# A recurrent attention kernel: value halves at both ends of the forward projections, and five unit buffers with one buffer of key rows in the backward loop

## The chip, the cores and the metric

The kernel runs on one core of a Trainium2 chip, as one program. The metric is the time of one execution on the device in microseconds (us). Five engines work beside each other, each through its own list of instructions in order, and wait for each other by semaphores: PE (matrix products into PSUM banks), DVE and ACT (elementwise work and copies out of PSUM), POOL (a general engine) and SP, which here only issues DMAs. DMAs are also issued from ACT and POOL. "PEld" in the profile is PE's loading of the stationary operand.

## The reference

The input x (2048 tokens, width 640) is normalised to xn. Branch A is attention in 64 segments of 32 tokens, with 32 heads of 128; ahead of each segment stand 8 memory rows, which are the first 8 output rows of the segment before. Branch B is a gated MLP of width 1728. The output is x + A * silu(B). The program also computes the gradients with respect to x, mem0 and all seven weights for a given grad_out.

```python
for s in range(n_seg):                      # 64 segments, one after the other
    h = concat([mem, xn[:, 32*s:32*s+32]])  # 8 memory rows + 32 rows
    q, k, v = h @ Wq, h @ Wk, h @ Wv        # 32 heads of 128
    p = softmax(where(mask, q @ k.T * scale, -1e9))
    o = (p @ v) @ Wo
    mem = o[:, :8]                          # goes into the next segment
    outs.append(o[:, 8:])
A = concat(outs)
B = (silu(xn @ w1) * (xn @ w3)) @ w2
out = x + A * silu(B)                       # and its gradients for grad_out
```

Only the 8 memory rows depend on the segment before. The 32 body rows of q, k and v of all segments can be projected beforehand, and their attention can be done in batches.

## The kernel before

The program runs through stages: layer norm, the body rows' projections and the MLP; the first rows; the forward loop over 64 segments (`recurrence`, inner function `chain(t)`); a tail; a prologue and the backward loop over the 64 segments in reverse (`phase4_Abwd`, inner function `chain(t)`); the weight gradients. The two loops are serial: a step ends when the 8 new memory rows (forward) or their gradients (backward), turned to columns, are cast into `hx` or `gox` for the next step.

**What sets the order.** In both loops every engine is tied to the order in which the program is written (`in_order`). Batch work on body rows is put into named gaps of the step (W0, W1, V0, W2, G1 to G6) by `FILL` (forward) and by `gap` in `gap_of` (backward). Its piece is a unit (tl, qd): four heads of three segments, 96 body rows and 24 memory rows, 120 in all. A step takes 3, 3 and 2 units in turn.

**A forward step.** `packed_half(bank, hx, W, b)` (L315) is half of one projection of the memory rows into a PSUM bank, 20 matmuls of 512 columns over 32 partitions each. The banks are bA, bB and bC. `half` casts the bank into a staging tile on DVE. The order on PE is: K half 0 (bA), K half 1 (bB), gap W0, Q half 0 (bA), Q half 1 (bB), the selection of the key columns (`packed_sel`, into bC, copied into `kT`), gap W1, the selection of the query columns (into bA), gap V0, V half 0 (bB), V half 1 (bC), gap W2, the scores (L672, bA), a turning of them (L682), the softmax of the memory rows on DVE and ACT (`mmx`, `msb`, `Pm`, L684 to L693), its turning on PE (`turn_pad`, L311), the product with the value rows `vt` (L701) and the output projection `packed_out` (L339) with `fold_add` and `fold_turn`, from which `hx` of the next step is cast (L718).

The staged halves have two uses. They are written to DRAM for the backward pass by `dump` on SP (L635): keys into KS, queries and values into QVS. And the 8 value rows of each of four groups are copied from the staging tile into `vt` (L663), six copies on DVE and two on POOL. The staging tiles have the tag "stg" with two buffers: keys, queries and values take them in turn, so that the value halves go into the buffer of the keys of the same step, once the key dump has read it. The tile `oride` holds the body rows' attention output, loaded in gap W0 by SP (L870) and copied into `oTm` by POOL in gap G1 (L875); its tag, "oride", has one buffer, which `fold_add` also uses at the end of the step.

**A backward step.** `load_k(t - 1)` (L1190) loads the 8 memory and 32 body rows of keys of the next step on SP by four DMAs (L1193, L1198). They go into one of two buffers by t % 2, `krbs`: a tile `krb` and `vt`. PE reads them at L1288. Each unit has the functions `ld` (L1315: queries, values and grad rows into a `gqv` and a `gor`, probabilities into a `gPr`), `turn` (L1341, turning on PE, L1347 and L1354), `dprob`, `dsoft` and `gmem`. NG = 4 sets of buffers hold units in flight; `gmem_ld` runs `gmem` of one unit and then `ld` of the next in the list, into the set that comes free. In the prologue two further buffers serve as sets, `krb` and `vt`, six in all.

## Time and profile before

| | us |
|---|---|
| median of 3 runs (lowest, highest) | 4638.5 (4625.86, 4665.23) |
| the profiled execution, its own time | 4653.07 |
| its span | 4651.3 |
| its granted TensorE clock, share of full | 0.979 |
| forward loop, first to last cast of hx | 402.1 to 1552.1 |
| backward loop, first to last cast of gox | 1819.6 to 2851.9 |

The span lies within the profiled execution's time, and the durations come from that one execution, 14.57 us above the median of the runs. A row of a busy table gives engine, busy time and number of instructions. A row of a wait table names the instruction that waited, what released it (the engine and tile, or a DMA and what it moved), the sum of the waits, their number and the longest. A row of a timeline gives start and duration in us, the engine, the line, the operation with tiles and shapes, and in brackets the idle time before it and its releaser; x6 stands for six instructions in one row, whose duration is that from the first to the last of them. A "SPq" or "ACTq" row is a DMA issue by that engine. Where the DMA issues of a step are listed, the last figure is the time from issue to landing.

The whole span by engine, and the costliest lines of the chain of work that ended last:

```profile
## 4 chain that ended last, share of the span: by engine, by line
PE 62%; DMA 7%; DVE 5%; issue 5%; ACT 4%; SPq 1%; POOL 1%; ACTq 0%; POOLq 0%; DVEq 0%
PE bank L339 12%; PE wg L1694 11%; PE g L1675 9%; PE bank L320 7%; PE oa L1841 4%; PE wa L2229 2%; PE r6p L1625 2%; PE t6g L1657 2%; PE w2a L2085 1%; PE bank L1260 1%; PE pgxb L2162 1%; DMA kTT<-GOS 1%; DMA ggtok<-ggT 1%; PE bank L672 1%; PE bank L1288 1%
```

L339 (`packed_out`) and L320 (`packed_half`) are the products of the memory rows in the two loops; L1694 and L1675 belong to the weight gradients, which the change does not touch.

### The profile page before, as it was taken

The numbers are of one execution on the slowest core, as the hardware profiler recorded it, in microseconds if no ns is written. First come the engines' busy times: TensorE is split into PE (matmuls) and PEld (weight loads), VectorE is DVE, ScalarE is ACT, GpSimd is POOL, SyncE is SP. The second block draws the span as 40 slices with busy tenths as digits, with TensorE's granted clock in tenths as the row PEclk, the third lists the DMA queues.
The fourth block names the chain that finished last, engine by engine and source line by source line (L and its number), as shares of the span: only waits on it lengthen the run. The fifth ranks groups of instructions, "written<-read, shape, count | busy, mean of one in ns | idle before, by whom it ended". The sixth has DMA issues, their size and how long they took to land.

```text
span 4651.3 us, 155619 instructions
## 1 busy us (share of the span) xinstructions
PE 4338.8 (93%) x62336; PEld 2841.2 (61%) x62336; DVE 2277.9 (49%) x7158; ACT 1616.0 (35%) x4487; POOL 2103.7 (45%) x3531
## 2 busy tenths in 40 slices
PE   8998999999999888999999998999999999999999
PEld 4544566666656545666666665676666765667665
DVE  8734676666667534555555553243223432311550
ACT  5532555555545423333333332233223322200000
POOL 6532555555555313455554544455335543311440
PEclk9998999999999998999999999999999999999999
DMA  7773666666655668787787775655435543588783
GB/s 262 240 253 108 177 184 186 182 185 188 183 168 172 165 162 238 206 227 220 220 222 208 213 214 154 134 159 141 118 105 155 153 131 110 161 229 206 164 174 101
DMA packets 976828, 834.52 MB, mean 179 GB/s; under 512 B 518890, under 2 KB 858286, under 8 KB 974144
## 3 DMA queue, kind: packets, MB, share of 16 engines
q1 hardware_dynamic: 745319, 530.80, 41.7%
q0 software_dynamic: 129952, 228.13, 17.1%
q10 hardware_dynamic: 100835, 65.63, 5.5%
q8 instruction: 493, 8.08, 0.8%
q14 instruction: 229, 1.88, 0.1%
HBM read 472.66 MB, written 310.33 MB: 168 GB/s over the span
## 4 chain that ended last, share of the span: by engine, by line
PE 62%; DMA 7%; DVE 5%; issue 5%; ACT 4%; SPq 1%; POOL 1%; ACTq 0%; POOLq 0%; DVEq 0%
PE bank L339 12%; PE wg L1694 11%; PE g L1675 9%; PE bank L320 7%; PE oa L1841 4%; PE wa L2229 2%; PE r6p L1625 2%; PE t6g L1657 2%; PE w2a L2085 1%; PE bank L1260 1%; PE pgxb L2162 1%; DMA kTT<-GOS 1%; DMA ggtok<-ggT 1%; PE bank L672 1%; PE bank L1288 1%
## 5 line engine op out<-in xcount | busy, mean ns | idle before, releaser
L1694 PE MATMUL wg<-gr,hr 128*128 128x512 bf16 x2400 | 521.7, 379 | 0.0
L1675 PE MATMUL g<-land,ghacc 128*128 128x320 bf16 x3072 | 459.0, 300 | 0.8
L320 PEld LDWEIGHTS <-hx 128*32 128x32 bf16 x10240 | 277.9, 97 | 254.1 <-issue 28.9
L1694 PEld LDWEIGHTS <-hr 128*128 128x128 bf16 x2400 | 233.9, 98 | 278.9
L1675 PEld LDWEIGHTS <-ghacc 128*128 128x128 bf16 x3072 | 288.7, 98 | 103.7 <-ACT ghacc L92 2.2
L90 DVE CAST wgo<-wg 128x512 bf16<-128x512 f32 x72 | 49.8, 692 | 471.2 <-PE wg L1694 471.2
L339 PEld LDWEIGHTS <-gkv 128*8 128x8 bf16 x8192 | 193.9, 89 | 89.8 <-issue 2.4
L92 ACT COPY ghacc<-t6g 128x768 bf16<-128x768 bf16 (+1 forms) x176 | 137.2, 780 | 292.6 <-PE t6g L1657 284.6
L90 DVE CAST stg<-bank 128x512 bf16<-128x512 f32 x256 | 177.0, 692 | 125.2 <-PE bank L320 111.1
L1640 POOL DMA_DIRECT2D GSP<-grs x48 | 25.6, 544 | 452.6 <-ACT grs L1632 452.6
L1351 POOL DMA_DIRECT2D VTD<-gvT x176 | 130.1, 748 | 216.6 <-ACT gvT L1350 201.1
L904 POOL DMA_DIRECT2D OR<-xv x163 | 94.5, 580 | 276.8 <-ACT xv L92 241.8
L663 DVE COPY vt<-stg 8x512 bf16<-8x512 bf16 x384 | 158.9, 414 | 97.3 <-ACT stg L92 92.9
L851 POOL TENSOR_TENSOR xP<-xP,xrz 120x480 bf16<-120x480 bf16 x163 | 161.4, 993 | 87.7 <-DVE xrz L850 77.9
L1681 DVE TENSOR_TENSOR ghacc<-ghacc,g 128x320 f32<-128x320 f32 x192 | 93.6, 487 | 209.0 <-PE g L1675 209.0
L92 ACT CAST wgo<-wg 128x512 bf16<-128x512 f32 x48 | 28.1, 586 | 479.8 <-PE wg L1694 392.5
L831 ACT ACTIVATE xP<-xsp,xnm 120x120 bf16<-120x120 f32 (+1 forms) x540 | 186.0, 367 | 19.7 <-DVE xnm L813 17.6
L339 PE MATMUL bank<-Wo,oTm 128*32 128x320 bf16 x4032 | 169.8, 327 | 15.8 <-DVE oTm L90 15.5
L339 PE MATMUL bank<-WvT,gkv 128*8 128x320 bf16 x4096 | 170.3, 325 | 0.0
L320 PE MATMUL bank<-WoT,hx 128*32 128x512 bf16 x2560 | 153.5, 386 | 11.3 <-DVE hx L1309 10.9
L1398 POOL DMA_DIRECT2D GXP<-gks x157 | 92.2, 587 | 154.4 <-ACT gks L1396 149.9
L351 ACT COPY fup<-bank 64x160 f32<-64x160 f32 (+1 forms) x190 | 57.3, 334 | 300.7 <-PE bank L339 300.4
(396 smaller groups left out, 10947.7 us busy)
## 6 DMA issues: line engine op xcount, KB each, us to landing
QVS<-stg SPq DMA_DIRECT2D x128, 256.0 KB
kTT<-VTD SPq DMA_DIRECT2D x64, 320.0 KB
PR<-xP POOLq DMA_DIRECT2D x168, 120.0 KB, 3.1
VTD<-gvT POOLq DMA_DIRECT2D x168, 120.0 KB, 4.1
land<-DSR SPq DMA_DIRECT2D x168, 120.0 KB
land<-PR SPq DMA_DIRECT2D x168, 120.0 KB
OR<-xv POOLq DMA_DIRECT2D x163, 120.0 KB, 3.6
orr<-OR SPq DMA_DIRECT2D x14, 1280.0 KB
```

Of the source, the lines that this page charges most:

```text
L90: return nc.vector.tensor_copy(out, in_)
L92: return nc.scalar.copy(out, in_)
L320: k.nc.tensor.matmul(bank[32 * g:32 * g + 32, :], x[:, dc, :], W[:, dc, c0:c0 + 512], start=(dc == 0), stop=(dc == k.DC - 1), tile_positio ...
L339: k.nc.tensor.matmul(pm[a][p0:p0 + nq, 0:320], x[:, h, :], W[:, h, 320 * b:320 * b + 320], start=(first and i == 0), stop=(last and i == 1 ...
L663: (nc.gpsimd if b == 1 and g % 2 else nc.vector).tensor_copy(vt[p0:p0 + 8, c0:c0 + 512], sv[32 * g:32 * g + 8, b * 512:(b + 1) * 512])
L831: nc.scalar.activation(Pb[0:n, j, 0:n], sp[0:n, j, :], ACT.Exp, bias=nmx[0:n, j:j + 1], scale=k.scale, accum_out=Z[0:n, j:j + 1])
L851: eng.tensor_tensor(Pb[0:n, :, 0:n], Pb[0:n, :, 0:n], bc_last(rz[0:n], n), ALU.mult)
L904: q.dma_start(k.OR[120 * tl:120 * tl + n, c0:c0 + 512], v[0:n])
L1351: nc.gpsimd.dma_start(k.VTD[tl][:, :, h0:h0 + 4, :], vTq[:])
L1675: nc.tensor.matmul(pg[:], ring[:, i, j, r0:r0 + P], Ws[qd][i][:, j, 320 * h:320 * h + 320], start=(i == 0 and j == 0), stop=(i == 2 and j ...
L1694: nc.tensor.matmul(pw[:], hr[:, tl, dc * P:(dc + 1) * P], grs[i][:, tl, :], start=(tl == 0), stop=(tl == NF - 1))
L1841: nc.tensor.matmul(ac[j][i][:], orr[:, w, jj * P:(jj + 1) * P], gow[:, w, 320 * i:320 * i + 320], start=(w == 0), stop=(w == NW - 1))
```

## The change

Forward, the value projection is cut in two. V half 0 is the first product of a step (bA); ACT casts it into a new tile `sv0`, which takes the "oride" buffer, and DVE copies its four groups of value rows between the two K casts. The K and Q halves follow in other banks. V half 1 comes last (bC), into the left half of a staging tile that is still the keys' one, and its four groups (two copies on DVE, two on POOL) follow. The halves are dumped apart: the first after gap W0, the second after the products with `vt`. The oride load moves from W0 to V0, behind the dump of `sv0`, whose buffer it takes. The copy of the turned keys into `kT` goes from DVE to ACT, and `kprep` of a third unit from ACT to DVE.

Backward, key rows always go to `vt`. The tile `krb` is replaced by a tile `ub` of the same size, which holds the `gqv`, `gor` and `gPr` of a fifth set, NG = 5; the prologue keeps six sets, with one more load in its last rounds.

```diff
--- before.py
+++ after.py
@@ -623,45 +623,49 @@
             hx = hxs[t % 2]
             kT = kTs[tl % 2]
 
-            def half(W, b, sg, eng):
-                bank = (bA, bB)[b]
+            def half(W, b, sg, bank):
                 packed_half(k, bank, hx, W, b)
-                k.copy(sg[:, b * 512:(b + 1) * 512], bank[:], eng=eng)
+                nc.vector.tensor_copy(sg[:, b * 512:(b + 1) * 512], bank[:])
 
             def stage():
                 return ch.tile([P, 1024], BF16, name="stg", tag="stg", bufs=2)
 
             def dump(sg, dst, q=nc.sync):
-                q.dma_start(dst.rearrange("g r c -> (g r) c"), sg[:])
+                q.dma_start(dst.rearrange("g r c -> (g r) c"), sg)
+
+            def values(b, sv, bank):
+                packed_half(k, bank, hx, Wv, b)
+                k.copy(sv, bank[:], eng='s')
+
+            def value_rows(b, sv):
+                for g in range(4):
+                    p0, c0 = 64 * (g // 2), (g % 2) * 1024 + b * 512
+                    (nc.gpsimd if b == 1 and g % 2 else nc.vector).tensor_copy(vt[p0:p0 + 8, c0:c0 + 512], sv[32 * g:32 * g + 8])
+            sv0 = ch.tile([P, 512], BF16, name="sv0", tag="oride")[:]
+            values(0, sv0, bA)
             sk = stage()
-            half(Wk_, 0, sk, 'v')
-            half(Wk_, 1, sk, 'v')
+            half(Wk_, 0, sk, bB)
+            value_rows(0, sv0)
+            half(Wk_, 1, sk, bC)
             gap("W0")
+            dump(sv0, k.QVS[t // 4, :, :, t % 4, 1, 0:512])
             sq = stage()
-            half(Wq, 0, sq, 'v')
-            dump(sk, k.KS[t // 4, :, :, t % 4])
-            half(Wq, 1, sq, 'v')
+            half(Wq, 0, sq, bA)
+            dump(sk[:], k.KS[t // 4, :, :, t % 4])
+            half(Wq, 1, sq, bB)
             qmT = ch.tile([P, H, 8], BF16, name="qmT", tag="fup")
-            for sg, b_, dst in ((sk, bC, kT[:, :, 40 * s:40 * s + 8]), (sq, bA, qmT[:])):
+            for sg, b_, dst, eng in ((sk, bC, kT[:, :, 40 * s:40 * s + 8], 's'), (sq, bA, qmT[:], 'v')):
                 pk = bview(b_, P, 8, 4, 8)
                 packed_sel(k, pk, sg, 0)
                 packed_sel(k, pk, sg, 1)
-                nc.vector.tensor_copy(dst.rearrange("p (g j) c -> p j g c", g=4), pk[:])
+                k.copy(dst.rearrange("p (g j) c -> p j g c", g=4), pk[:], eng=eng)
                 if sg is sk:
                     gap("W1")
-            dump(sq, k.QVS[t // 4, :, :, t % 4, 0])
+            dump(sq[:], k.QVS[t // 4, :, :, t % 4, 0])
             gap("V0")
-            sv = stage()
-            packed_half(k, bB, hx, Wv, 0)
-            k.copy(sv[:, 0:512], bB[:], eng='s')
-            packed_half(k, bC, hx, Wv, 1)
-            for b in range(2):
-                if b == 1:
-                    k.copy(sv[:, 512:1024], bC[:], eng='s')
-                for g in range(4):
-                    p0, c0 = 64 * (g // 2), (g % 2) * 1024 + b * 512
-                    (nc.gpsimd if b == 1 and g % 2 else nc.vector).tensor_copy(vt[p0:p0 + 8, c0:c0 + 512],
-                                                                               sv[32 * g:32 * g + 8, b * 512:(b + 1) * 512])
+            sv1 = stage()[:, 0:512]
+            values(1, sv1, bC)
+            value_rows(1, sv1)
             gap("W2")
 
             psT = bview(bA, P, 2, 8, 16)
@@ -702,7 +706,7 @@
             om_ = oTm[:].rearrange("p (a b j) t -> p a b j t", a=2, b=2)
             for i in range(2):
                 k.copy(om_[:, :, i, :, 0:8], poms[i].rearrange("p j a q -> p a j q"), eng='vs'[i])
-            dump(sv, k.QVS[t // 4, :, :, t % 4, 1])
+            dump(sv1, k.QVS[t // 4, :, :, t % 4, 1, 512:1024])
             if t + 1 == T:
                 gap("G4")
                 gap("G5")
@@ -943,16 +947,15 @@
 
         def FILL(g, t, at, kbatch):
             kb = kbatch.get(t, ())
-            if g == "W0":
-                oride_ld(t)
-            elif g == "W1":
+            if g == "W1":
                 for u in kbatch.get(t - 1, ())[2:]:
-                    kprep(*u)
+                    kprep(*u, 'v')
                 at(pv_mm, t - 1, 1)
                 at(pv_turned, t - 1, 1)
                 at(turn_p, t - 1, 2)
             elif g == "V0":
                 at(pv_rows, t - 1, 1)
+                oride_ld(t)
             elif g == "W2":
                 ride_ld(t + 1)
                 for u in kb[0:2]:
@@ -1131,29 +1134,29 @@
                       k.FS[k.OT0:k.OT0 + k.NO, 32 * b + 8:32 * b + 32, :]))
     with tc.tile_pool(name="gst", bufs=1) as st, tc.tile_pool(name="gchain", bufs=1) as ch, \
             tc.tile_pool(name="gfill", bufs=1) as fl:
-        NG = 4
+        NG = 5
         kTs, vt, goxs, qTs, xPs, PTs, oTm = own
         kk = k.kTT
         om = oTm[:].rearrange("p h c -> p (h c)")
         two = lambda ap: ap.rearrange("p (i c) -> p i c", i=2)
         four = lambda ap: ap.rearrange("p (i c) -> p i c", i=4)
-        gors = [kk[0:120, 512 * i:512 * i + 512] for i in range(NG)]
-        gqvs = [two(ap[0:120, c:c + 1024]) for ap, c in ((kk, 2048), (kk, 4896), (kk, 5920), (om, 0))]
+        ub = st.tile([P, 2048], BF16, name="ub")
+        gors = [kk[0:120, 512 * i:512 * i + 512] for i in range(4)] + [ub[0:120, 1024:1536]]
+        gqvs = [two(ap[0:120, c:c + 1024]) for ap, c in ((kk, 2048), (kk, 4896), (kk, 5920), (om, 0), (ub, 0))]
         vTf = kk[:, 3584:4896]
         vTb = vTf[:, 0:1280].rearrange("p (h c) -> p h c", c=40)
         Qsts = [two(kk[:, c:c + 256]) for c in (3072, 3328)]
-        gPrs = [four(kk[0:120, 6944:7456])] + [x[0:120] for x in xPs]
+        gPrs = [four(kk[0:120, 6944:7456])] + [x[0:120] for x in xPs] + [four(ub[0:120, 1536:2048])]
         dSb = kk[:, 7456:7648]
         gOTs = qTs[0:2]
         gdSs = [qTs[2][0:120], PTs[0][0:120]]
         bds = [PTs[1][:, 2 * i:2 * i + 2, :].rearrange("p a (h c) -> p a h c", c=8) for i in range(2)]
-        krbs = [st.tile([P, 2048], BF16, name="krb")[:], vt[:]]
         k.fsz = st.tile([P, 448], BF16, name="gfsz")
         bdm = st.tile([P, 16, 8], BF16, name="bdm")
         b16 = st.tile([P, 16], F32, name="b16")
         xpb = st.tile([P, 8, 2, 32], F32, name="xp")
         bdf = goxs[0][:, 0:4, :].rearrange("p a b -> p (a b)").rearrange("p (a b) -> p a b", b=8)
-        for tt in gors + [t[:] for t in gOTs] + gdSs + [dSb, krbs[0], k.fsz[:]]:
+        for tt in gors + [t[:] for t in gOTs] + gdSs + [dSb, ub[:], k.fsz[:]]:
             nc.vector.memset(tt, 0.0)
         bA, bB, bC = banks
         pm = bA, bA
@@ -1188,7 +1191,7 @@
             ins[t] = vT, Pm, Qst
 
         def load_k(t):
-            kr = krbs[t % 2]
+            kr = vt[:]
             for a in range(2):
                 nc.sync.dma_start(kr[64 * a:64 * a + 8].rearrange("r (g c) -> r g c", g=2),
                                   k.KS[t // 4, 2 * a:2 * a + 2, 0:8, t % 4, :].rearrange("g r c -> r g c"))
@@ -1324,7 +1327,7 @@
                 gor = gors[g]
                 qv, Pr = gqvs[g], gPrs[g]
             else:
-                x = krbs[g - NG]
+                x = vt
                 qv = x[:, 0:1024].rearrange("p (i c) -> p i c", i=2)
                 gor = x[:, 1024:1536]
                 Pr = x[:, 1536:2048].rearrange("p (h c) -> p h c", h=4)
@@ -1495,7 +1498,7 @@
         next(work)
         for _ in range(2):
             ld_next()
-        nc.vector.memset(krbs[1][:, 1024:1536], 0.0)
+        nc.vector.memset(vt[:, 1024:1536], 0.0)
         ld_next()
         for i in range(len(pro) + 2):
             for f, o in ((turn, 0), (dprob, 1), (dsoft, 1), (gmem, 2)):
@@ -1503,7 +1506,7 @@
                     f(*pro[i - o])
                 if f is not dsoft and not (f is dprob and i % 3):
                     next(work, None)
-            if 0 <= i - 2 and (i - 2 + 6 < len(pro) or i >= len(pro) - 2):
+            if 0 <= i - 2 and (i - 2 + 6 < len(pro) or i >= len(pro) - 3):
                 ld_next()
             if 1 <= i < 17:
                 h0 = 2 * (i - 1)
```

DVE in a forward step, from the first cast of a projection to the maximum of the memory scores. bank_4107, bank_4108 and bank_4109 are bA, bB and bC. Before:

```order
L90 CAST stg<-bank_4107 128x512
L90 CAST stg<-bank_4108 128x512
L90 CAST stg<-bank_4107 128x512
L90 CAST stg<-bank_4108 128x512
L649 CAST kTT<-bank_4109 128x8x4x8
L865 COPY xPT_2984<-xpp 120x4x120
L649 CAST qmT<-bank_4107 128x8x4x8
L663 COPY vt<-stg 8x512 x6
L684 TENSOR_REDUCE mmx<-bank_4107 128x2
```

And now:

```order
L628 CAST stg<-bank_4108 128x512
L643 COPY vt<-sv_23267 8x512 x4
L628 CAST stg<-bank_4109 128x512
L628 CAST stg<-bank_4107 128x512
L628 CAST stg<-bank_4108 128x512
L90 COPY kTT<-kpt 128x12x32
L869 COPY xPT_2984<-xpp 120x4x120
L90 CAST qmT<-bank_4107 128x8x4x8
L643 COPY vt<-stg 8x512 x2
L688 TENSOR_REDUCE mmx<-bank_4107 128x2
```

Four of the six value-row copies have moved ahead of the second K cast, two are left ahead of the maximum; the key cast into kTT has gone to ACT, and the copy of a unit's keys (kpt) has come.

SP in the same step, from its first issue to the loads of a unit's keys; in brackets what each waits for (a DMA lane, or an engine's count). Before:

```order
L870 DMA oride<-OTX 128x768 [waits DMAHW2_49,DVE_49]
L635 DMA KS<-stg 128x1024 [waits DMAHW3_49,DVE_49]
L635 DMA QVS<-stg 128x1024 [waits DMAHW4_49,DVE_49]
L265 DMA kr<-KS 96x512 [waits DMAHW6_49]
L265 DMA kr<-KS 96x512 [waits DMAHW7_49,PE_49]
```

And now:

```order
L634 DMA QVS<-sv_21799 128x512 [waits DMAHW7_49,Activation_49]
L634 DMA KS<-stg 128x1024 [waits DMAHW0_49,DVE_49]
L634 DMA QVS<-stg 128x1024 [waits DMAHW1_49,DVE_49]
L874 DMA oride<-OTX 128x768 [waits DMAHW7_49,DMAHW3_49,Pool_49]
L265 DMA kr<-KS 96x512 [waits DMAHW4_49]
L265 DMA kr<-KS 96x512 [waits DMAHW5_49,PE_49]
```

The oride load has moved from the first place to behind both dumps, and it now waits for the landing of the dump of `sv0` and for POOL too.

SP in a backward step, from the load of the memory queries to the store of the score gradients. Before:

```order
L1187 DMA kTT<-QM 128x1x128 [waits DMAHW0_49]
L1193 DMA krb<-KS 8x2x1024 [waits DMAHW1_49]
L1198 DMA krb<-KS 32x2x1024 [waits DMAHW2_49]
L1193 DMA krb<-KS 8x2x1024 [waits DMAHW3_49]
L1198 DMA krb<-KS 32x2x1024 [waits DMAHW4_49]
L1299 DMA DSR<-kTT 8x16x8 [waits DMAHW5_49,DVE_49]
```

And now:

```order
L1190 DMA kTT<-QM 128x1x128 [waits DMAHW4_49]
L1196 DMA vt<-KS 8x2x1024 [waits DMAHW5_49,PE_49]
L1201 DMA vt<-KS 32x2x1024 [waits DMAHW6_49]
L1196 DMA vt<-KS 8x2x1024 [waits DMAHW7_49]
L1201 DMA vt<-KS 32x2x1024 [waits DMAHW0_49]
L1302 DMA DSR<-kTT 8x16x8 [waits DMAHW1_49,DVE_49]
```

The key loads stand at the same place and go to `vt` in every step; the first of them now waits for PE, which reads the rows of the step it is issued in.

## The prediction

> **What bounds the kernel now.** I read first the busy shares and the two loop headers, which cut the span into stages; then the busy table of the two loops; then what PE waits for in them; last the timeline of single steps. PE is busy for 93% of the span, and the change touches the two recurrent loops alone.
>
> ```profile
> PE 4338.8 (93%) x62336; PEld 2841.2 (61%) x62336; DVE 2277.9 (49%) x7158; ACT 1616.0 (35%) x4487; POOL 2103.7 (45%) x3531
> ...
> L718 DVE CAST hx<-bank x63: 198/200/200, 402.1 to 1552.1; 128x40 bf16<-128x40 f32 x63
> ...
> L1309 DVE CAST hx<-bank x63: 198/200/201, 1819.6 to 2851.9; 128x40 bf16<-128x40 f32 x63
> ```
>
> The cast of hx that ends a step stands 63 times from 402.1 to 1552.1 (forward) and from 1819.6 to 2851.9 (backward): 62 steps of 18.55 us and 62 of 16.65 us. In the busy table (sum and count of each engine, then granted clock, DMA share, GB/s) both stretches show PE at 92% and a clock of 0.98:
>
> ```profile
> 402.10:1552.10 1150.00, 1058.62 (x20717) 693.50 (x20718) 782.92 (x2106) 603.42 (x1970) 637.16 (x993) 0.98 0.62 176
> 1819.60:2851.90 1032.30, 952.11 (x22619) 665.71 (x22619) 553.06 (x2814) 355.88 (x1219) 504.46 (x914) 0.98 0.74 208
> ```
>
> So only two things can be had without less work for PE: its waits, and the 2% of clock, 23 us (0.02 x 1150) forward and 20 us backward (clock lost between half and full rate, taken as time). The waits (us in all, count, longest), forward first, then the backward ones that end with a unit's loads:
>
> ```profile
> PE bank L311 <- DVE Pm L693: 54.0, 62, 2.6
> ...
> ACT stg L92 <- DMA KS<-stg: 10.1, 11, 2.2
> ```
>
> ```profile
> PE ggpt L1354 <- DMA kTT<-GOS: 6.1, 7, 1.4
> ...
> PE gvpt L1347 <- DMA kTT<-QVM: 4.7, 3, 3.0
> ...
> PE ggpt L1354 <- DMA kTT<-GX: 2.5, 3, 1.4
> PE gvpt L1347 <- DMA kTT<-QVX: 2.4, 3, 1.9
> ...
> PE gvpt L1347 <- DMA kTT<-QVS: 1.3, 3, 0.7
> ```
>
> Forward PE stands once in each step at the turning of the memory softmax (L311), 54.0 us in all. In 11 steps ACT stood before that, because the value staging takes the slot that the key dump to DRAM is still reading. Backward, 19 waits for unit loads make 17.0 us. A short wait can cost more than itself: one of 0.84 us at 1888.5 is followed by a packed_out (L339) of 4.02 us, against 2.35 us elsewhere.
>
> ```profile
> 1888.48 0.38 PE L1354 MATMUL ggpt<-ident,kTT 120*128 120x120 bf16 x4 [0.84 <-DMA kTT<-GX]
> 1891.13 4.02 PE L339 MATMUL bank<-WvT,gkv 128*8 128x320 bf16 x64
> ...
> 2393.92 2.35 PE L339 MATMUL bank<-WvT,gkv 128*8 128x320 bf16 x64
> ```
>
> **The forward step.** A step without a late DMA begins at 1128.58 (times from there: +). Duration stands second, idle time and its releaser in brackets.
>
> ```profile
> 1128.58 0.20 DVE L718 CAST hx<-bank 128x40 bf16<-128x40 f32 x1
> 1130.46 0.69 DVE L90 CAST stg<-bank 128x512 bf16<-128x512 f32 x1 [0.41 <-PE bank L320]
> 1131.55 1.00 POOL L851 TENSOR_TENSOR xP<-xP,xrz 120x480 bf16<-120x480 bf16 x1
> 1132.26 0.34 SPq L635 DMA_DIRECT2D KS<-stg  x1
> 1133.70 0.69 DVE L90 CAST stg<-bank 128x512 bf16<-128x512 f32 x1 [0.39 <-PE bank L320]
> 1136.79 2.51 DVE L663 COPY vt<-stg 8x512 bf16<-8x512 bf16 x6 [1.28 <-ACT stg L92]
> 1137.25 0.59 ACT L92 CAST stg<-bank 128x512 bf16<-128x512 f32 x1 [0.49 <-PE bank L320]
> 1137.89 1.25 POOL L663 COPY vt<-stg 8x512 bf16<-8x512 bf16 x2 [0.89 <-ACT stg L92]
> 1138.58 0.22 PE L682 MATMUL bank<-ident,sTm 128*128 128x40 bf16 x2
> 1139.33 0.24 DVE L684 TENSOR_REDUCE mmx<-bank 128x2 f32<-128x80 f32 x1
> 1139.44 0.82 POOL L875 COPY oTm<-oride 128x768 bf16<-128x768 bf16 x1
> 1140.95 0.29 PE L311 MATMUL bank<-ident,Pm 128*128 128x128 bf16 x2 [0.50 <-DVE Pm L693]
> ...
> L663 DVE COPY vt<-stg x384: 280/288/821, 389.0 to 1561.7; 8x512 bf16<-8x512 bf16 x192
> ```
>
> What is to be seen: the scores stand ready at +10.22 (L682 ends 1138.80), but DVE begins their maximum (mmx) only at +10.75, since six value-row copies of 2.51 us stand ahead. From mmx on a chain of small DVE and ACT steps leads to L311, where PE loses 0.50.
>
> After the change the four K and Q halves come one place later; their spacing is (5.12 - 1.88) / 3 = 1.08 us, from the first and last of the four casts. The second value half ends where it ended (the same matmuls stand ahead of it), so its cast stays at +8.67 to +9.26. DVE then has two copies instead of the rest of six: one of 0.29 (the row's median 288 ns) and one beside POOL's two, as the last two now, (2.51 - 4 x 0.29) / 2 = 0.68. mmx moves to 9.26 + 0.03 + 0.29 + 0.68 = +10.26, just behind the scores. **Calm steps: at most -0.45 each**, -22 over 50 of them. The moved work lies beside matmuls: the four early copies (1.16 us) between two casts on DVE, the key transpose's copy on ACT, which is free there. I take -12 for them, about half, because steps have other last waits (ACT, below). Bounds 0 and -22.
>
> **The key dump, the price of it.** Now it is issued at +3.68 and its slot wanted by ACT at +7.6 (the cast of 0.59 that releases the copies at +8.21 began there): 3.9 us are allowed. After: first K cast +2.96 to +3.65; the copies behind it run into POOL's 1.00 us at +2.97 to +3.97 and end near +5.0 (an estimate; at +4.8 without); second K cast to +5.7; dump at about +5.75. The slot is now wanted for the second value half, at +8.67. **2.9 us are allowed; each us beyond delays mmx one for one**, so a landing of 2.9 + 0.5 = 3.4 us gives back the whole gain of a calm step. A late step shows the worst of them (the chain's rows: start, us):
>
> ```profile
> 1312.66 0.39 SPq L870 DMA_DIRECT2D oride<-OTX  x1
> ```
>
> ```profile
> 1313.52 4.93 DMA KS<-stg
> ...
> 1318.55 0.59 ACT stg L92
> ...
> 1322.29 0.25 DVE mmx L684
> ```
>
> There the 768-column oride load went out on SP 0.86 us ahead of the dump, and the dump took 4.93. The change moves that load behind both dumps. With the same 4.93 the step would not be worse than now: 2.07 later issued, but only two copies follow, mmx at +5.75 + 4.93 + 0.59 + 1.0 = +12.3, as now (1322.29 with hx at 1310.06). I take the landing at or below 3.4 in most steps, nearer to the 3.1 us of the page's 120 KB writes than to 4.93, since 51 of 62 steps show no wait at an allowance of 3.9:
>
> ```profile
> PR<-xP POOLq DMA_DIRECT2D x168, 120.0 KB, 3.1
> ```
>
> **Late steps:** of the 10.1 us on 11 steps I take 8 back, bounds 0 and -10. **Clock:** L311's waits are what PE stands for in this loop; with them cut to about a third I take 10 of the 23 us, bounds 0 and -16; the rival without it is below.
>
> **ACT late:** the new first cast on ACT feeds the value rows, and they now stand ahead of the second K cast. In some steps ACT is still busy then:
>
> ```profile
> 925.61 0.20 DVE L718 CAST hx<-bank 128x40 bf16<-128x40 f32 x1
> ...
> 927.37 0.48 ACT L92 CAST xoT<-xot 128x384 bf16<-128x384 f32 x1 [1.48 <-DMA OTX<-xoT]
> ...
> 928.45 0.59 ACT L92 CAST xv<-xpo 120x512 bf16<-120x512 f32 x1 [0.60 <-DMA PR<-xP]
> ```
>
> ACT is free at +3.43, so the value cast ends at +4.0 rather than +2.5, and everything of K on DVE comes near 1 us later: half of it lost, on some 13 steps (one in five, an estimate), **+7**, bounds 0 and +20. **oride:** its load is issued about +7.5 in the place of the first SP issue of the step, and POOL's copy, now at +10.86, waits for it by some 0.4; PE needs oTm only 2 us later. **+3** with the one DMA more on SP (0.34 each, behind no wait), bounds 0 and +8. Forward: -12 - 8 - 10 + 7 + 3 = **-20**, bounds -48 to +28 without the dump's case below.
>
> **Backward.** A unit's loads now start one unit earlier, about a third of a step or 16.65 / 3 = 5.5 us. A load of the grad rows issued on ACT's queue at 2403.26 was used 4.1 us later:
>
> ```profile
> 2397.10 0.67 PE L1288 MATMUL bank<-gdST,krb 128*128 128x16 bf16 x16 [0.23 <-ACT gdST L312]
> 2398.36 0.48 SPq L1193 DMA_DIRECT2D vt<-KS  x1
> ...
> 2403.26 0.73 ACTq L265 DMA_DIRECT2D kTT<-GOS  x1
> 2407.40 0.37 PE L1354 MATMUL ggpt<-ident,kTT 120*128 120x120 bf16 x4
> ```
>
> That lead becomes about 10 us, and the longest wait was 3.0, so all 19 go: -17.0. Of the 20 us of clock I take 15, nine such groups at 4.02 - 2.35 = 1.67 each. The single key-row buffer makes the next key load wait for L1288 of this step; that ends at 2397.77, before the load's issue at 2398.36, and its reader stands a step, some 16 us, later: nothing, or 0.48 per step at most if SP were held. The clearing of the new buffer and one unit more in flight ahead of the loop: +2. Backward: -17 - 15 + 2 = **-30**, bounds 0 to -37.
>
> **Sum.** -20 - 30 = -50 on the profiled execution of 4653.07 (span 4651.3): 4603. The median of the runs shown, 4638.5, is 14.6 lower, so 4588.
>
> **Rivals.** (1) *The forward stall goes whole*: dumps land within 2.9 us everywhere, the late steps and L311's 0.45 go in all 62 (-28), with 10 and 10 for late steps and clock: -48 forward, -32 backward, 4558. For it: the dump no longer stands behind oride; against it: 11 of 62 steps whose dump landed later than 3.9. The Trainium skill, "DMA: Bandwidth & Descriptors", Anatomy of one DMA — SWDGE (gpsimd) path, fits 2.0 us plus bytes / 436e3; as an estimate that is 2.6 us for 256 KB and would give this case, but the 4.93 above and 3.1 for 120 KB stand well over it. (2) *Five buffers do not help*: the loads are limited by the queues (DMA share 0.74 in that loop), start earlier and land no earlier: backward 0, forward -20, 4618. (3) *No clock comes back*: the slow groups fall where they fall, and shorter waits leave their number as it is; without the 10 and the 15 the sum is -25, 4613. Against it: the 0.84 us right ahead of the slow group at 1891.13. The Trainium skill, "TensorE: Matmul & The Clock Gate", Part 1: The HAM clock gate, has the array fall to half rate only after an idle window of about 3.4 us, which none of these waits reaches, and so stands with this rival; the row disagrees. (4) *The key dump ends the value half in many steps*: mean landing 3.7, so 0.3 of loss per step, forward +20, backward -30: 4628. (5) *Slower*: the dump, issued beside the V0 dump and the unit loads, takes the 4.93 in every step: (4.93 - 3.4) x 62 = +95, with -30 backward 4703. It decides from a mean landing of 3.4 + 30 / 62 = 3.9 us on.
>
> **How the numbers follow.** About 1% (46 us: 4592 and 4685) is what a measurement of this kernel can tell from no change. The forecast, 4588, holds 0.45 with 4572 to 4605, of which 0.27 below 4592; rival 1 0.16, rival 2 0.08, rival 3 0.07, rival 4 0.15 (4605 to 4650), rival 5 0.09. Faster 0.27 + 0.16 = 0.43; same 0.18 + 0.08 + 0.07 + 0.15 = 0.48; slower 0.09. The range 4552 to 4642 leaves out rival 5 and the outer ends of 1 and 4, about 0.2.
>
> **What will show it.** Right: backward no waits at L1354 and L1347 for loads and a clock of 0.99 or more; forward L311's waits at 20 us or less, mmx at +10.3 in a calm step. Wrong: ACT's wait for KS on many steps (rivals 4 and 5), a mean step above 18.55; waits for kTT or ub unchanged (rival 2); a clock still at 0.98 with the waits gone (rival 3); new waits of POOL for oride that reach L339.

## The result, and the profile after

| | before | changed | ratio, 95% interval |
|---|---|---|---|
| median us (lowest, highest) | 4647.86 (4625.86, 4665.23) | 4608.16 (4602.07, 4624.73) | 0.9921 (0.9901 to 0.9941) |
| runs | 9 | 9 | |
| the profiled execution | 4653.07 | 4624.73 | |
| its forward loop | 1150.0 | 1145.8 | |
| its backward loop | 1032.3 | 1003.9 | |

The change is worth 0.79%, some 37 us (0.0079 x 4647.86; 27 to 46 by the interval): less than the 50 forecast, and short of the 46 us that were called the bound of what can be told from no change. The time lies in the range and the direction was right. The two loops in the busy table of the changed kernel (length, then busy time and count of PE, its weight loads, DVE, ACT and POOL, then clock, DMA share, GB/s):

```profile
400.70:1546.50 1145.80, 1036.46 (x20593) 682.33 (x20717) 756.71 (x2085) 604.96 (x1990) 642.56 (x993) 0.99 0.62 177
1815.10:2819.00 1003.90, 938.66 (x22616) 663.30 (x22619) 553.61 (x2814) 352.90 (x1219) 505.01 (x914) 0.99 0.76 214
```

In this trace records of 124 of PE's forward instructions are missing, two in each step: filler products that stand ahead of L311 and of the folding. Its PE waits are therefore too long, at L311 by some 0.3 us in a step ((36.5 - 19.5) / 62, the sum here less that of e9), and are not set against those of before. The traces of e1 to e4 lack as many. The same kernel was profiled once more as e9, with the full count of 20717, the count of before; its rows serve instead:

```profile
394.77:1528.37 1133.60, 1047.14 (x20717) 678.90 (x20718) 755.40 (x2085) 604.53 (x1990) 639.80 (x991) 0.99 0.62 178
1796.48:2804.23 1007.75, 943.69 (x22619) 665.18 (x22619) 553.74 (x2814) 353.10 (x1219) 503.30 (x914) 0.99 0.76 213
```

PE's waits there, forward (sum, count, longest):

```profile
PE bank L311 <- DVE Pm L697: 19.5, 31, 1.5
PE bank L339 <- DVE oTm L90: 14.6, 50, 0.8
PE xpp L868 <- POOL xP L855: 10.7, 20, 2.0
PE bank L328 <- DVE stg L628: 9.7, 19, 0.8
PE bank L686 <- ACT sTm L678: 7.8, 28, 1.0
PE bank L705 <- ACT PTm L312: 4.8, 7, 1.2
PE bank L320 <- ACT sv L92: 3.3, 7, 0.7
```

The wait at L311 fell from 54.0 to 19.5 us, by 34.5. But PE now waits in four places where it hardly waited before. Of these the old rows were:

```profile
PE bank L328 <- DVE stg L90: 1.7, 8, 0.4
PE xpp L864 <- POOL xP L851: 1.0, 5, 0.3
PE bank L701 <- ACT PTm L312: 0.7, 2, 0.4
```

L868 +9.7, L328 +8.0, L705 +4.1 and L320 +3.3 make 25 us: some three quarters of the gain at L311 stand there again. Backward, the 19 waits for unit loads (17.0 us) are gone; what is left of a unit's loads is this:

```profile
PE bank L1291 <- DMA ub<-QVM: 0.2, 1, 0.2
PE bank L1291 <- DMA kTT<-GOS: 0.2, 1, 0.2
```

A calm step of the changed kernel, without a wait for the key dump, begins at 1074.25 in its first trace:

```profile
1074.25 0.20 DVE L722 CAST hx<-bank 128x40 bf16<-128x40 f32 x1
1077.20 1.00 POOL L855 TENSOR_TENSOR xP<-xP,xrz 120x480 bf16<-120x480 bf16 x1
1077.22 0.69 DVE L628 CAST stg<-bank 128x512 bf16<-128x512 f32 x1 [1.49 <-PE bank L320]
1077.82 1.43 DVE L643 COPY vt<-sv 8x512 bf16<-8x512 bf16 x4
1080.00 0.34 SPq L634 DMA_DIRECT2D KS<-stg  x1
1082.92 0.59 ACT L92 CAST stg<-bank 128x512 bf16<-128x512 f32 x1
1084.58 0.24 DVE L688 TENSOR_REDUCE mmx<-bank 128x2 f32<-128x80 f32 x1
1085.70 0.82 POOL L879 COPY oTm<-oride 128x768 bf16<-128x768 bf16 x1 [0.41 <-DMA oride<-OTX]
1085.90 0.72 DVE L697 TENSOR_TENSOR Pm<-Pm,rZm 128x80 bf16<-128x80 bf16 x1
1086.67 0.28 PE L311 MATMUL bank<-ident,Pm 128*128 128x128 bf16 x2 [0.77 <-DVE Pm L697]
```

The places are those worked out beforehand: first K cast at +2.97, key dump at +5.75, last value cast at +8.67, maximum at +10.33 (forecast +2.96, +5.75, +8.67, +10.26). And yet L311 waits 0.77 us here (some 0.3 less, were the filler ahead of it on record), for another reason: the softmax, being earlier, now runs beside POOL's copy of oride, which is later because its load is; and DVE's last softmax step, Pm, takes 0.72 us instead of 0.24. A step in which the same lateness is worse begins at 679.6:

```profile
687.35 0.38 SPq L874 DMA_DIRECT2D oride<-OTX  x1
...
692.65 0.82 POOL L879 COPY oTm<-oride 128x768 bf16<-128x768 bf16 x1 [1.82 <-DMA oride<-OTX]
...
698.43 1.94 POOL L855 TENSOR_TENSOR xP<-xP,xrz 120x480 bf16<-120x480 bf16 x2
...
699.48 0.38 PE L868 MATMUL xpp<-ident,xP 120*128 120x120 bf16 x4 [2.77 <-POOL xP L855]
```

POOL stands 1.82 us for oride, everything behind it in its written order comes later, and at the end PE waits 2.77 us for the norm of a unit. (POOL also stood 1.76 us at a store between the two, so the 2.77 are not the load's alone.) A second load is late in the same way, the body rows of x (`ride`, loaded every fourth step by SP right behind oride). These are POOL's waits, in the kernel before for ride alone (its copy of oride had no wait listed), then in e9 for both:

```profile
POOL hx L619 <- DMA ride<-XN: 6.0, 7, 1.7
```

```profile
POOL hx L619 <- DMA ride<-XN: 22.6, 14, 2.8
POOL oTm L879 <- DMA oride<-OTX: 11.5, 14, 1.9
```

### The profile page after: what moved, and what is told of

Read it like the earlier page. It is cut to its first block, busy times and chain, and to the rows that moved or that the text cites. A ratio compares the mean times of both kernels' runs of the same rounds, so it can differ in the third digit from the quotient of the medians.

```text
span 4623.0 us, 155683 instructions
## 1 busy us (share of the span) xinstructions
PE 4302.4 (93%) x62114; PEld 2828.5 (61%) x62336; DVE 2251.9 (49%) x7137; ACT 1615.4 (35%) x4509; POOL 2110.7 (46%) x3531
## 5 line engine op out<-in xcount | busy, mean ns | idle before, releaser
L320 PEld LDWEIGHTS <-hx 128*32 128x32 bf16 x10240 | 266.5, 97 | 264.7 <-issue 27.5
L855 POOL TENSOR_TENSOR xP<-xP,xrz 120x480 bf16<-120x480 bf16 x163 | 163.8, 1020 | 49.2 <-DVE xrz L854 39.4
L339 PE MATMUL bank<-Wo,oTm 128*32 128x320 bf16 x4032 | 159.2, 313 | 15.3 <-DVE oTm L90 14.1
L320 PE MATMUL bank<-WoT,hx 128*32 128x512 bf16 x2560 | 154.1, 388 | 11.3 <-DVE hx L1312 10.9
L320 PE MATMUL bank<-Wv,hx 128*32 128x512 bf16 x2560 | 161.6, 381 | 1.1 <-DVE hx L722 1.1
L245 POOL DMA_DIRECT2D land<-QVS x256 | 144.9, 570 | 30.4 <-DMA land<-GOS 5.8
```

Source lines behind the costliest of these rows:

```text
L245: eng.dma_start(d, src if src.shape[0] > 1 else src[0])
L320: k.nc.tensor.matmul(bank[32 * g:32 * g + 32, :], x[:, dc, :], W[:, dc, c0:c0 + 512], start=(dc == 0), stop=(dc == k.DC - 1), tile_positio ...
L339: k.nc.tensor.matmul(pm[a][p0:p0 + nq, 0:320], x[:, h, :], W[:, h, 320 * b:320 * b + 320], start=(first and i == 0), stop=(last and i == 1 ...
L855: eng.tensor_tensor(Pb[0:n, :, 0:n], Pb[0:n, :, 0:n], bc_last(rz[0:n], n), ALU.mult)
```

## The experiments

Each run was timed beside the kernel before on the same chip; ratios are to that, with the 95% interval.

### The two halves of the change

e1 is the changed forward loop with the backward loop of before, e2 the reverse; their edits are the two parts of the change's diff.

> The forward half of the change alone, with the backward loop of before. Theory A (the two halves add up: forward loop 1150.0 to 1145.8 us, backward 1032.3 to 1003.9 in the two profiles): 3 to 12 us faster than before, ratio 0.997 to 0.9995, with PE's waits at the turning of a unit's probabilities (xpp from xP) still near 15 us in the forward loop and the backward loop at 1030 or more. Rival B (the forward half gains nothing, and what it showed is the spread between executions): ratio 0.999 to 1.003.

Measured: 4625.65 us, ratio 0.9976 (0.9963 to 0.999), about 11 us, as theory A had it. PE waited 11.8 us for xP, where some 15 were expected, and the backward loop of before took 1027.6 us here, a little under the bound named.

> The backward half of the change alone (five unit buffers, one buffer of key rows), with the forward loop of before. Theory A: 25 to 33 us faster than before, ratio 0.993 to 0.995, the backward loop at about 1004 us with no waits of PE for unit loads. Rival B (part of the 28 us came from the state that the forward loop leaves): 10 to 20 us, ratio 0.996 to 0.998.

Measured: 4622.86 us, ratio 0.9961 (0.9945 to 0.9978), about 18 us, backward loop 1010.9 us. The size is that of rival B, but not its reason: the backward loop of before took 1032.3 us in the first profile, 1027.6 in e1 and 1024.3 in e4, so that the 28 us between the first two profiles compared a long execution with a short one. The halves give 0.9976 x 0.9961 = 0.9937, within the interval of the whole.

### The oride load, early again

```diff
-            sv0 = ch.tile([P, 512], BF16, name="sv0", tag="oride")[:]
+            sv0 = ch.tile([P, 512], BF16, name="sv0", tag="fup")[:]
...
-            if g == "W1":
+            if g == "W0":
+                oride_ld(t)
+            elif g == "W1":
...
                 at(pv_rows, t - 1, 1)
-                oride_ld(t)
```

> The changed kernel with the first value half staged in another buffer (the one of fup) and the oride load put back into gap W0, ahead of the dumps. Theory A (the late oride load holds POOL, whose norm then comes late for PE's turning of the probabilities, xpp from xP): POOL's waits for oride fall from 14.0 us to under 3, PE's waits for xP from 15.2 to under 4, and the forward loop loses another 15 to 25 us, about 4588 in all, ratio to before 0.985 to 0.989. Rival B (POOL is late because of the value rows that DVE now copies beside its norm): waits for xP stay at 12 us or more and the time at about 4608, ratio 0.991 to 0.993. Rival C (the load ahead of the dumps makes the key dump slow again, above 2.9 us): ACT waits for KS on more than 15 steps, and the gain is under 8 us.

Measured: 4594.3 us, ratio 0.9895 (0.9876 to 0.9913). The waits did what theory A said (PE's for xP 3.8 us); of the time it got 12 us by the ratios (0.9921 - 0.9895), not 15 to 25. e11 is the same kernel again, beside e9, the changed kernel:

> The changed kernel itself, beside the next three on one chip, so that their distances are measured against it. All theories: ratio to before 0.990 to 0.994.

> e3 again beside the changed kernel. Theory A (the late load costs 10 us or more): 8 to 18 us below the changed kernel of the same call. Rival B (e3 came out low by the spread between chips): under 5 us.

Measured on one chip: e9 4610.32 us, ratio 0.992 (0.9902 to 0.9938); e11 4596.81 us, ratio 0.9895 (0.9874 to 0.9917): 13.5 us below. The intervals of the ratios overlap in both comparisons, but both give about the same distance, and the ten runs with the load early (e3, e11) lie between 4580.6 and 4602.8 us, the 21 with it late (the changed kernel, e9, e10) between 4598.2 and 4624.7. The waits of PE and POOL in e11:

```profile
PE xpp L868 <- POOL xP L855: 4.0, 10, 1.0
...
POOL hx L619 <- DMA ride<-XN: 11.8, 10, 2.3
```

POOL's copy has no wait for oride listed any more, its wait for ride is halved, and PE's for xP fell from 10.7 to 4.0 us. So the late loads were a part of what the change gave back.

e10 takes the early load away again but keeps the other buffer, and so parts the place of the load from the wait for the shared buffer:

```diff
-            sv0 = ch.tile([P, 512], BF16, name="sv0", tag="oride")[:]
+            sv0 = ch.tile([P, 512], BF16, name="sv0", tag="fup")[:]
```

> The changed kernel with the first value half in the buffer of fup, as in e3, but the oride load left where the change put it, in gap V0. It parts the two things that e3 took back at once: the place of the load and its wait for the first value dump. Theory A (the place does it: issued at about +7.5, when the value dump has long landed): POOL's waits for oride 9 us or more, PE's for xP 9 or more, time within 4 us of the changed kernel. Rival B (the shared buffer does it): both waits near those of e3 (under 4), time near e3, 8 to 15 us below the changed kernel.

Measured: 4609.28 us, ratio 0.9928 (0.9909 to 0.9947), 1.0 us from e9:

```profile
PE xpp L868 <- POOL xP L855: 10.6, 20, 2.5
...
POOL oTm L879 <- DMA oride<-OTX: 12.2, 15, 1.6
```

Both waits are as in e9. It is the place of the load in SP's order, not the buffer.

e4 moves the load in the kernel before and does nothing else:

```diff
-            if g == "W0":
-                oride_ld(t)
-            elif g == "W1":
+            if g == "W1":
...
                 at(pv_rows, t - 1, 1)
+                oride_ld(t)
```

> The kernel before, with one thing moved: the oride load from gap W0 to gap V0, behind both dumps. Theory A: POOL waits for oride 10 us or more, PE for xP 8 us or more where it was about 1, and the key dump lands faster (the 11 waits of ACT for KS, 10.1 us, go): the two nearly cancel, -8 to +10 us, ratio 0.998 to 1.002. Rival B (the load's place does not touch PE): no new waits for xP and only the gain by the key dump, 8 to 20 us, ratio 0.9955 to 0.998.

Measured: 4630.9 us, ratio 0.9981 (0.9969 to 0.9994), about 9 us faster, at the edge of both expectations. Theory A was wrong in the waits:

```profile
POOL oTm L875 <- DMA oride<-OTX: 1.9, 4, 0.8
...
ACT stg L92 <- DMA KS<-stg: 3.1, 3, 1.1
...
PE xpp L864 <- POOL xP L851: 1.6, 5, 0.5
```

The same gap is not the same time. Here the dumps ahead of the load go out early, and so does the load:

```profile
1093.67 0.20 DVE L718 CAST hx<-bank 128x40 bf16<-128x40 f32 x1
...
1099.88 0.69 SPq L870 DMA_DIRECT2D oride<-OTX  x1
```

That is +6.2, against +7.4 in the changed kernel's step at 1074.25 (SP issued it at 1081.62); 1.2 us later POOL's waits for it are 11.5 us in e9 and not 1.9. It also shows what the load's old place had cost: behind both dumps, ACT's waits for the key dump are 3.1 us, against 10.1 in the first profile, 7.4 in e2 and 5.6 in e8, which all have the forward loop of before. About as much as the whole forward half gained (11 us) comes with moving this one load.

### POOL's copy beside the softmax

e5 is e3 with POOL's copy of oride moved ahead of the value rows:

```diff
             elif g == "V0":
+                oride(t)
                 at(pv_rows, t - 1, 1)
...
             elif g == "G1":
-                oride(t)
```

> e3 with one thing more: POOL's copy of oride into oTm moved from gap G1 to gap V0, ahead of POOL's value rows, so that it is over before the memory softmax. Theory A (the earlier maximum runs the softmax into POOL's copy, and DVE's last step, Pm, is held while POOL copies: 0.242 us alone, up to 0.65 in the 48 of 64 steps of e3 that overlap): no overlap, Pm at 0.24 in every step, PE's wait at L311 from 34.2 us to 20 to 27, and 6 to 15 us off e3, ratio to before 0.986 to 0.988. Rival B (Pm's length is not on the path that ends the step): L311 as in e3 and the time within 3 us of it, 0.989 to 0.990.

Measured: 4590.17 us, ratio 0.9902 (0.9882 to 0.9921). Pm and the waits:

```profile
L697 DVE TENSOR_TENSOR Pm<-Pm,rZm x64: 241/243/364, 391.4 to 1528.5; 128x80 bf16<-128x80 bf16 x64
```

```profile
PE bank L311 <- DVE Pm L697: 15.3, 25, 1.5
PE bank L328 <- DVE stg L628: 9.5, 25, 0.8
...
POOL oTm L879 <- DMA oride<-OTX: 50.2, 34, 4.0
```

The longest Pm fell from 903 ns (in e9) to 364; the time did not follow. There was little to be had: the 34.2 us that the expectation set out from are of e3's trace, which lacks the filler products; e11, the same kernel with the full count, has 17.9 us at L311, and there all Pm together are longer than 0.242 us each by 2.8 us (27 of 64 steps; in e9 by 4.2 us in 21). Nor is it a test of Pm alone: POOL's copy now stands 50.2 us for its load, and it runs while DVE copies the value rows; the wait at L328 stays.

e6 gives the first value cast to DVE, e7 puts the first value rows behind the second K cast; both start from e5:

```diff
-            values(0, sv0, bA)
+            packed_half(k, bA, hx, Wv, 0)
+            nc.vector.tensor_copy(sv0, bA[:])
```

> e5 with the first value half cast by DVE and not by ACT. Theory A (ACT is still busy with units when that half is ready, and what waits for it on DVE, the value rows and the second key cast, comes late): PE's waits for the key staging at L328 (8.9 us in the changed kernel) fall under 3, its waits for sTm (10 to 12 us) under 9, and 5 to 12 us go. Rival B (DVE, 0.69 us fuller in each step, becomes late itself): waits as before and 0 to 10 us slower than e5.

Measured: 4587.29 us, ratio 0.9897 (0.9876 to 0.9917). PE's wait for the key staging was 10.3 us and that for sTm 11.2, where under 3 and under 9 were expected: without ACT's cast the key staging is as late. The cast now takes DVE's own time, though, as rival B had it, so that this alone does not clear ACT. What the late steps have in common is seen in the traces. One of e9:

```profile
1023.90 0.20 DVE L722 CAST hx<-bank 128x40 bf16<-128x40 f32 x1
...
1027.38 0.59 ACT L92 CAST sv<-bank 128x512 bf16<-128x512 f32 x1
...
1028.00 2.42 DVE L643 COPY vt<-sv 8x512 bf16<-8x512 bf16 x4 [0.45 <-ACT sv L92]
1028.39 0.99 POOL L855 TENSOR_TENSOR xP<-xP,xrz 120x480 bf16<-120x480 bf16 x1
...
1031.20 0.35 PE L328 MATMUL bank<-sel,stg 128*128 128x32 bf16 x8 [0.84 <-DVE stg L628]
```

In 28 of the 62 steps of e9 the four value-row copies run beside POOL's norm (L855) and take 1.35 to 2.38 us together; in the other 34 no work of POOL runs beside them and they take 1.14 at most. All of PE's idle time right ahead of the first selection (L328), 8.0 us, falls in the 28. In 8 of the 11 steps that lose over 0.15 us there (6.6 of the 8.0 us) DVE had first stood for ACT's cast, as above; in e11 in 6 of 13 (4.9 of 9.1), in e5 in one of 10 (0.8 of 5.4). So the late steps share that the copies meet work of POOL, and a late ACT, which moves the copies into the norm, is a part of it: the larger one in e9, the smaller in e5.

e12 is e6 again, beside e9 and e11:

> e6 again (load early, POOL's copy early, first cast on DVE) beside e11 and the changed kernel. If Pm's 0.05 to 0.4 us beside POOL's copy is on the path: 3 to 10 us below e11. If what the copy gave up at the softmax comes back at the value rows on DVE (four copies of 1.17 us alone, up to 1.8 beside POOL) and at L328: within 3 us of e11.

Measured: 4593.27 us, ratio 0.9896 (0.9875 to 0.9918), 3.5 us under e11 and no difference in the ratio: the two further edits are worth nothing that can be told.

```diff
-            value_rows(0, sv0)
             half(Wk_, 1, sk, bC)
+            value_rows(0, sv0)
```

> e5 with the four first value-row copies written behind the second key cast, and not ahead of it; ACT keeps the first cast. Theory A (a late ACT cast holds the value rows, and these the key cast): L328's waits for the key staging under 3 us and the key dump issued 1 to 1.5 us earlier, at +4.3; ACT's waits for KS under 3 us; 4 to 10 us off e5. Rival B (the rows then hold the query casts instead): L328's waits unchanged, time within 3 us of e5.

Measured: 4600.04 us, ratio 0.9922 (0.9904 to 0.9941), 10 us over e5, though the intervals overlap. ACT's wait for the key dump went to none, but L328 rose:

```profile
PE bank L328 <- DVE stg L628: 13.5, 41, 0.5
```

The four copies now hold the query casts in 41 places. Ahead of the keys or behind them, they take DVE's time between two casts that PE waits for; rival B, and slower than it said.

### One buffer of key rows

e8 is the kernel before with the backward loop's key rows always in `vt` and four unit sets:

```diff
-            kr = krbs[t % 2]
+            kr = krbs[1]
```

> The kernel before with only the key rows of the backward loop changed: one buffer for all steps, four unit sets as before. Theory A (the load is issued after its buffer's last reader anyway): same as before, ratio 0.9985 to 1.0015, backward loop 1024 to 1032 us. Rival B (the load waits for PE on SP and holds what is queued behind it): 5 to 25 us slower, ratio 1.001 to 1.0055.

Measured: 4647.72 us, ratio 1.0026 (1.0006 to 1.0047), about 12 us slower. SP's own waits show a new first row:

```profile
SPq L1193 <- PE bank L1288: 72.2, 46, 3.5
```

In the timeline, a step of the kernel before and one of e8:

```profile
2380.62 0.75 SPq L1193 DMA_DIRECT2D krb<-KS  x1
...
2380.98 0.68 PE L1288 MATMUL bank<-gdST,vt 128*128 128x16 bf16 x16
```

```profile
2369.17 0.68 PE L1288 MATMUL bank<-gdST,vt 128*128 128x16 bf16 x16
2369.88 0.30 SPq L1193 DMA_DIRECT2D vt<-KS  x1
```

Before, SP issued the key load ahead of the product that reads the other buffer, and in the whole loop 53 of 63 such loads ahead of the product's end; now it stands until that product is over, and with it the stores and unit loads queued behind. The changed kernel has the wait too (51.6 us, 33 times, in its trace). What two buffers of key rows would give beside five unit sets was not tried.

## Why the prediction came out as it did

**The whole.** -37 us against -50, of which the forward loop gave about 11 where 20 were forecast and the backward loop about 18 where 30 were. The measured 4608 lies in the wide range, but above the band that the forecast gave itself (4572 to 4605) and in that of rival 4, whose reason, a slow key dump, the waits do not show. Of its 20 us above 4588, 9 are the median of before, which stood at 4638.5 in three runs and at 4647.86 in nine. The busy tables part the rest, PE's idle time being a loop's length less PE's busy time, first profile against e9:

| us | forecast | first profile to e9 |
|---|---|---|
| forward, idle (the terms without the clock) | -12 - 8 + 7 + 3 = -10 | 91.4 to 86.5, -4.9 |
| forward, busy (the clock) | -10 | 1058.6 to 1047.1, -11.5 |
| backward, idle (without the +2, part of it ahead of the loop) | -17 | 80.2 to 64.1, -16.1 |
| backward, busy (the clock) | -15 | 952.1 to 943.7, -8.4 |

Both mechanisms were right. Short came out the forward waits, where two prices were sized too small, and the clock backward. These differences add up to -41 and not to -37 because the first profile is a long execution.

**Forward, calm steps and the key dump: right.** The order and the places came as worked out, the maximum at +10.33 instead of +10.26. The dump was the open price, and it fell to the cheap side: in e9 no wait of the value cast is put down to KS (in the first profile of the changed kernel 5 are, 9.2 us), so that it landed within the 2.9 us allowed in nearly all steps, against 11 waits before at an allowance of 3.9. That is the condition of the first rival; a landing as late as the fifth's 4.93 us came in single steps at most (the longest of the 5 waits is 2.7 us). The fit of the Trainium skill ("DMA: Bandwidth & Descriptors", Anatomy of one DMA — SWDGE (gpsimd) path) gave 2.6 us as an estimate for these 256 KB; it is stated for DMAs issued from POOL, and this dump is issued from SP. The absent waits agree with it here, but they only bound the landing, by 2.9. L311's waits ended at 19.5 us, as said.

**Forward, oride: a step that failed.** It was taken at +3, bounds 0 and +8, because "PE needs oTm only 2 us later". That looked at one reader. POOL's order has the softmax's stores and a unit's norm behind that copy, and PE waits for the norm: +9.7 us at L868, and the copy also slid beside Pm. The load of ride, pushed back on the same queue, was not counted at all, though every load behind the dumps moves with them. e3, e10 and e11 show the price: 12 to 13.5 us come back when the load alone is early.

**Forward, ACT late: inside its bounds, at twice its size, and in part for another reason.** +7 was taken, bounds to +20; L328, L705 and L320 made 15 us. ACT was late as said (DVE stood 10 times for its cast, 6.4 us, in e9). What was mis-sized is the meeting of the four copies with POOL's norm: the prediction let them end 0.2 us later for it, and in the 28 steps that have it they took up to 1.24 us longer (2.38 against 1.14), and PE's 8.0 us ahead of L328 all fall there. e7 puts the copies elsewhere, and they hold the query casts instead.

**Clock: right in kind, full forward, short backward.** With equal counts of instructions, PE's busy time fell by 11.5 and 8.4 us, where 10 and 15 were taken. One pair of executions is a weak witness: the forward loop of before, run again in e8, had a busy time of 1048.77 us with the full count. The clock itself is a better one. The mean granted clock of the runs rose from 0.980 (28 runs of the kernel before) to 0.985 (9 runs of the changed one), with 0.983 in e1 and 0.982 in e2; counted as the prediction did, 0.0053 x 4639 is 25 us, the 25 that were taken in all. In the traces that run the forward loop of before (the first, e2, e8) the clock stood at half rate in 13, 11 and 9 stretches of it; in those of the changed one (its first, e1, e9) in 8, 5 and 3. So the third rival fell. No wait of PE in the rows shown reaches 3.4 us, so the rule of an idle window of about that length ("TensorE: Matmul & The Clock Gate", Part 1: The HAM clock gate, of the Trainium skill) does not describe these losses. That the shorter waits are the cause is an inference from their going together; no run changed the clock alone.

**Backward, five sets: right.** All waits of PE at the turning of a unit's loads went, -17.0. The second rival fell.

**Backward, one key buffer: wrong in the mechanism, its price here open.** It was taken at nothing, from one step in which the load was issued after PE had ended. That step was one of 10 in 63: at 2380.62 the load went out ahead of the product, and in 46 steps of e8 SP waited for it. The upper bound named, SP held in every step, was the truth in kind, and e8 prices it at 12 us (3 to 22) with four sets. With five sets SP is held as well, but PE has no wait for key rows listed in e9, and its idle time fell by 16 of the 17 us forecast, so no loss of PE's can be put down to it there. How much it costs with five sets is open.

## What to carry to other kernels

When a wait ahead of a serial chain is cut, list what else ran in that time: here three quarters of the gain at L311 were waited for elsewhere, behind a POOL whose load came later and behind DVE copies that now met POOL's norm. A load's place is set by what stands ahead of it in its queue, not by the gap it is written in, so when dumps move back, each load behind them has to be followed to the last reader of the engine that waits for it. Whether a new buffer wait is free is a question to all steps, not to one: compare the issue with the reader over the loop (the queue engine's own waits show it after).

A version faster than both kernels is e3: it moves one load and one buffer of the changed kernel, and stood at ratio 0.9895 in both of its measurements, 0.25 points under the changed kernel's 0.992; the further edits of e5 and e6 stay between 0.9896 and 0.9902.

## What the runs showed of the hardware

DVE's softmax step on a tile of 80 bf16 columns takes 0.242 us alone, and up to 0.903 us while POOL copies 128x768 bf16 beside it (in the step shown it ended 0.1 us after that copy; in e9 all 21 long ones run beside it); no such step exceeded 0.375 us once the copy was elsewhere (e5, e12). The 512-column copies of 8 rows are longer beside POOL's norm of 1.00 us in the same way: four take 1.35 to 2.38 us in e9, against 4 x 0.285 = 1.14 by their median. This agrees with the Trainium skill, "SBUF — State Buffer", SBUF: two separate sides, which has the two engines share a port that one holds for a whole instruction.

In the first profile PE's clock was granted at half rate in stretches of 3.41 us or twice that in the two loops, and not after idle time alone: it was 0.50 from 1891.51 to 1894.92, while PE had been busy for 2.79 of the 3.41 us ahead of that, at a clock of 1.00.
